# The last 96 columns of w1 join wqkv's third head block, and a table sets the order of all operations

## The chip, the cores and the metric

The kernel runs on one core of one Trainium2 chip. The metric is the device time of one execution in microseconds (us), from which the median of several runs is told. PE is TensorE, DVE VectorE, ACT ScalarE, POOL GpSimd and SP SyncE, whose queue issues every DMA of this kernel.

## The reference

With x of 2048 tokens by 512 channels, all in fp32:

```
xn = layernorm(x)                          # over the 512 channels
q, k, v = split(xn @ wqkv)                 # 32 heads of 16 channels
logits[s, w] = q[s] . k[s - 2*w] / 4       # a window of 8 keys, 2 apart; -1e9 before the start
s = softmax(logits) @ v, heads joined, @ wo
y = layernorm(xn)
g = silu(gelu(y @ w1 + b1) @ w2 + b2)      # w1: 512 x 1376, w2: 1376 x 512
out = x + s * g
```

1376 hidden channels are ten blocks of 128 and a last block of 96.

## The kernel before

**Arithmetic and tiles.** Each fp32 operand of a large product is split in two fp16 tiles, a high and a low part, and three of the four products of parts are summed, so each product takes three fp16 matmuls per 128 input channels (12 for 512). The tokens are dealt in two halves c = 0, 1 (even and odd positions), each of 8 tiles i of 128 tokens; `yT[0..3]` hold the normalised tokens transposed, 512 tokens each. The heads are taken in four head blocks hb of 8 heads, so there are eight units u = 4c + hb.

**A unit.** `qkv(c, hb, u)` (line 721) makes q, k and v of the unit: for each of the 8 token tiles, 12 matmuls with 128 tokens as the loaded operand and 384 streamed columns of `wq` (L746) fill one PSUM tile `ps`, which ACT (L763) or DVE (L759) scales into `U[u % 2]`. `attention(c, hb, u)` (line 790) works on DVE: four multiplies q by k (L805), four reductions (L808), a softmax, four multiplies by v (L863), adds on DVE (L858) and POOL (L873, L883). `U` has two buffers, so unit u+2's results can be written only after unit u's last L863.

**The channel MLP.** `mlp1(ch, f)` (line 1008) makes hidden block f for the 512 tokens of chunk ch: 12 matmuls with 128 columns of w1 loaded and 512 tokens streamed (L1016), then the gelu with its bias (ACT, L1033), the high part (ACT, L1036) and the low part (DVE, L1038). The last block f = 10 has 96 columns and goes into its own tile `hlast`, whose 97th row holds the constant for b2. Its matmuls stream 512 tokens as the others do. `mlp2(ch, f)` (line 1043) adds h times w2 into four PSUM tiles z, 3 matmuls of 512 columns each (L1052); after f = 10 ACT takes the silu (L1068), which goes to DRAM (`gd`). `mlp2` runs two steps behind `mlp1` (`LAG`).

**Start.** The first loads bring x (some tiles transposed, `xt`), wqkv of head block 0 (`stq`, in two halves) and w1. Token tiles 6 and 7 skip the normalisation for unit 0: `center` subtracts the mean, made by PE (L599) or by DVE and PE (L602, L608), and `direct` multiplies them in fp32 (L617). The others are normalised (`y0`: POOL L665, ACT L661 or DVE L668 by `Y_ENG`) and transposed by PE (L683) or, where `BYDMA` says so, by a DMA transpose (L675). 24 matmuls on a constant (L1169) fill PE meanwhile and compute nothing that is used.

**End.** `wo_last` (line 951) multiplies the second half's attention by wo: for each tile 9 matmuls over three head blocks, 3 more once the last block is there (L961). DVE multiplies by the gate (L993) and adds x (L1000; three tiles on POOL, L997), and a DMA writes the tile.

**Order.** `Plan` records every operation with what it reads and writes, and a cost. Before, `issue` (line 221) is a list scheduler: it repeatedly takes the operation that can start first by those costs, ties going by the priorities `PQ0`, `PY`, `PG` and others. Each engine runs its own list strictly in that order.

## Time and profile before

| | |
|---|---|
| median of 3 runs | 415.07 us (414.49 to 415.13) |
| the profiled execution, its own time | 415.18 us |
| its span, first to last instruction | 413.4 us, so 1.78 us lie around it |
| PE busy | 405.9 us, 98% of the span |
| DVE busy | 379.5 us, 92% |
| ACT, POOL busy | 222.1 us (54%), 120.3 us (29%) |
| mean granted PE clock | 0.999 |

A row of a timeline gives start, length, engine, line, operation, output <- input, how many instructions, and in brackets the idle time just before them and what ended it. A row of a group gives busy time, the mean of one in ns, then idle time and its releaser. Matmuls are pipelined, so the mean of one matmul in a group contains the overlap with its neighbours; their real rate is read from the chain, where a row gives the time that a run of them took.

### The profile page before, as it was taken

Reading aid. Unit: us, or ns where it says so; the run is one execution under the profiler, and the core shown is the slowest. Engines: PE = TensorE matmul, PEld = TensorE weight load, DVE = VectorE, ACT = ScalarE, POOL = GpSimd, SP = SyncE. Lnnn points to the kernel's source line nnn. Section 1 sums busy time; section 2 is a strip of 40 time slices with the busy share of each in tenths; the row PEclk is TensorE's granted clock in tenths of the full one; section 3 lists DMA queues with packets and bytes.
Section 4 is the critical chain, followed back from the end, with each engine's and each line's share of the span. In section 5 each row is a group of like instructions: output and inputs, shape, how many; then the busy total and the mean of one; then the engine's idle time right before and its main releaser. Section 6 shows DMA issues by size and latency. Waiting matters only on the chain.

```text
span 413.4 us, 5554 instructions
## 1 busy us (share of the span) xinstructions
PE 405.9 (98%) x2083; PEld 206.6 (50%) x2083; DVE 379.5 (92%) x379; ACT 222.1 (54%) x353; POOL 120.3 (29%) x131
## 2 busy tenths in 40 slices
PE   8799999999999999999999999999999999999996
PEld 5555544445654455445544554455455544444443
DVE  4996989998999999989998999999999998999954
ACT  4699899994549655843384252225212393263500
POOL 3834002004380425042504330434033404520021
PEclk9999999999999999999999999999999999999999
DMA  8958717030045137720172034223604244007133
GB/s 281 397 112 258 235 61 230 0 128 1 1 142 152 28 93 183 149 46 2 48 221 75 0 102 116 68 86 88 205 7 122 88 111 145 0 18 238 23 102 131
DMA packets 47211, 46.41 MB, mean 112 GB/s; under 512 B 31785, under 2 KB 32225, under 8 KB 46673
## 3 DMA queue, kind: packets, MB, share of 16 engines
q1 hardware_dynamic: 47184, 46.06, 37.6%
q8 instruction: 16, 0.26, 0.3%
q14 instruction: 11, 0.08, 0.1%
HBM read 24.06 MB, written 7.34 MB: 76 GB/s over the span
## 4 chain that ended last, share of the span: by engine, by line
PE 92%; ACT 3%; issue 1%; DVE 1%; POOL 1%; ACTq 0%
PE z L1052 28%; PE ps L1016 28%; PE ps L746 25%; PE ps L929 5%; PE ps L961 2%; PE z L961 2%; PE pl L746 1%; ACT w L421 1%; PE pl L961 1%; ACT f L673 1%; ACT yT L687 0%; ACT wq L536 0%; POOL wq L471 0%; POOL rb L635 0%; ACT prod L661 0%
## 5 line engine op out<-in xcount | busy, mean ns | idle before, releaser
L1016 PE MATMUL ps<-yT,w 128*128 128x512 f16 (+1 forms) x528 | 120.4, 379 | 0.0
L746 PE MATMUL ps<-wq,yT 128*128 128x384 f16 x708 | 117.0, 326 | 0.2 <-DVE U L759 0.2
L1052 PE MATMUL z<-w,h 128*128 128x512 f16 x480 | 110.4, 379 | 0.0
L746 PEld LDWEIGHTS <-yT 128*128 128x128 f16 x744 | 72.5, 98 | 49.2 <-issue 1.0
L1016 PEld LDWEIGHTS <-w 128*128 128x128 f16 (+1 forms) x528 | 52.8, 100 | 61.0
L805 DVE TENSOR_TENSOR prod<-U 128x2048 f32<-128x2048 f32 x32 | 73.2, 2286 | 2.2 <-POOL prod L883 0.7
L1052 PEld LDWEIGHTS <-h 128*128 128x128 f16 x480 | 46.6, 98 | 55.5 <-issue 0.3
L808 DVE TENSOR_REDUCE L<-prod 128x128 f32<-128x2048 f32 x32 | 73.0, 2281 | 0.4
L1033 ACT ACTIVATE ps<-ps,b1T,hsc 128x512 f32<-128x512 f32 (+1 forms) x44 | 32.9, 748 | 73.4 <-PE ps L1016 72.2
L863 DVE TENSOR_TENSOR prod<-pl,U 128x2048 f32<-128x2048 f32 x28 | 63.2, 2283 | 4.2 <-POOL prod L873 4.1
L763 ACT ACTIVATE U<-ps,cs 128x384 f32<-128x384 f32 x54 | 31.2, 580 | 65.2 <-PE ps L746 65.2
L873 POOL TENSOR_TENSOR prod<-prod,prod 128x2048 f32<-128x2048 f32 x7 | 31.7, 4531 | 113.8 <-DVE prod L863 99.6
L883 POOL TENSOR_TENSOR prod<-prod 128x1024 f32<-128x1024 f32 x14 | 32.9, 2349 | 0.0
L882 POOL COPY gate<-prod 1x1 f32<-1x1 f32 x21 | 5.5, 264 | 91.0 <-DVE prod L805 82.2
L1038 DVE SCALAR_TENSOR_TENSOR h<-ps,hsc,h 128x512 f16<-128x512 f32 x40 | 29.6, 741 | 1.7 <-ACT h L1036 1.4
L1036 ACT ACTIVATE h<-ps,hsc 128x512 f16<-128x512 f32 x40 | 27.3, 684 | 1.3 <-PE z L1052 0.4
L929 PE MATMUL ps<-wo,oT 128*128 128x512 f16 x96 | 21.7, 379 | 0.0
L858 DVE TENSOR_TENSOR prod<-prod,prod 128x2048 f32<-128x2048 f32 x9 | 20.5, 2282 | 0.0
L1033 ACT ACT_TABLE_LOAD x10 | 12.8, 1283 | 8.6 <-PE ps L1016 8.5
L883 POOL TENSOR_TENSOR prod<-prod,prod 128x1024 f32<-128x1024 f32 x7 | 16.4, 2347 | 0.0
L961 PEld LDWEIGHTS <-oT 128*128 128x128 f16 x108 | 10.6, 98 | 10.4
L929 PEld LDWEIGHTS <-oT 128*128 128x128 f16 x96 | 9.4, 98 | 11.2
(179 smaller groups left out, 377.8 us busy)
## 6 DMA issues: line engine op xcount, KB each, us to landing
f<-in_A_x_dram SPq DMA_DIRECT2D x31, 256.0 KB, 3.5
U<-U SPq DMA_DIRECT2D x16, 392.0 KB, 4.0
gd<-f SPq DMA_DIRECT2D x12, 256.0 KB, 3.4
prod<-in_A_x_dram SPq DMA_DIRECT2D x8, 256.0 KB, 6.9
oT<-in_B_w_dram SPq DMA_DIRECT2D x2, 1024.0 KB
yT<-in_B_w_dram SPq DMA_DIRECT2D x2, 1024.0 KB, 7.9
f<-gd SPq DMA_DIRECT2D x8, 256.0 KB, 2.7
out_dram<-f SPq DMA_DIRECT2D x8, 256.0 KB, 2.8
```

What stands on the lines that cost most here:

```text
L746: nc.tensor.matmul(b.t[:, 0:384], y[:, s, k, o:o + P], wq[:, hb, t, k], start=(n == 0), stop=(n == 11))
L763: act(384, lambda i=i, b=b: nc.scalar.activation(U3[:, i:i + 31:15, :], b.t[:, 0:384].rearrange("p (t e) -> p t e", t=3), AF.Identity, sca ...
L805: dve(2048, lambda p2=p2, g=g: nc.vector.tensor_tensor(p2(), q, slots(Ut, KH, 2 * g), op=ALU.mult), qk + [("kh", ub, 0), ("kh", ub, 1), (" ...
L808: dve(2048, lambda pr=pr, g=g: nc.vector.tensor_reduce(L3()[:, 2 * g:2 * g + 2], pr.t.rearrange("p (r f d) -> p r f d", r=2, d=DH), AX.X, ...
L863: dve(2048, lambda: nc.vector.tensor_tensor(pr.t.rearrange("p (r f d) -> p r f d", r=2, d=DH), A3()[:, 2 * g:2 * g + 2].rearrange("p r (f ...
L873: pool(4.75, lambda: nc.gpsimd.tensor_tensor(acc.t, acc.t, p1.t, op=ALU.add), [acc, p1], [acc])
L883: nc.gpsimd.tensor_tensor(x.t[:, 0:1024], x.t[:, 0:1024], y(), op=ALU.add)
L929: nc.tensor.matmul(b.t, oT[:, hb, i // 4, s, i % 4], wo[:, t, hb], start=(hb == 0 and n == 0), stop=(hb == last and n == 2))
L961: nc.tensor.matmul(b.t[:, cols], oT[:, hb, i // 4, s, i % 4], wo[:, t, hb, cols], start=(start and hb == 0 and n == 0), stop=(stop and hb ...
L1016: nc.tensor.matmul(b.t[0:M], w1[:, s, f * 512 + k * M:f * 512 + (k + 1) * M], yT[ch][:, t, k], start=(n == 0), stop=(n == 11))
L1033: act(512, lambda: nc.scalar.activation(b.t[0:M], b.t[0:M], AF.Gelu_apprx_tanh, bias=b1T[0:M, f:f + 1], scale=hsc[0:M, 1:2]), [b, ("b1T",) ...
L1052: nc.tensor.matmul(z.t, hl[s][0:K, t * P:(t + 1) * P], w2[0:K, w, f], start=(f == 0 and n == 0), stop=(f == NF - 1 and n == 2))
```

## The change

**The last block of w1.** `wq` becomes one tile per head block, and that of the third block (`HLAST = 2`) is 480 columns wide: 384 of wqkv and the 96 of w1. In units 2 and 6 the 12 matmuls of a token tile stream 480 columns. `mlp1` no longer runs for f = 10. Instead ACT copies the 96 extra columns of each tile out of PSUM into `hpt`, and `last_block`, once per chunk, adds the bias on POOL, takes the gelu and the high part on ACT and the low part on DVE. All this is by tokens, so a DMA transpose turns it into `hlt`, which `mlp2(ch, 10)` reads in place of `hlast`. `hlt` uses one new tile, `hl0`, and the tile `first`, where the constants of the start had been. b1 is loaded with 96 more columns.

**The order.** A table `ORDER` of 1260 numbers is followed by `issue` in place of its choice. Several settings change with it: which engine does which split, eviction or normalisation, the grouping of the first tiles, the load order, and the places of the MLP steps between units (`MLPN`).

```diff
+HLAST = 2
-BYDMA = (4, 5, 6, 7)
+BYDMA = (2, 5, 6, 7)
-Y_ENG = ('pool', 'act', 'dve', 'dve', 'act', 'pool', 'dve', 'act')
+Y_ENG = ('act', 'dve', 'act', 'dve', 'act', 'act', 'dve', 'act')
-W1ENG = ('act', 'dve', 'act', 'act', 'act', 'act', 'act')
+W1ENG = ('dve', 'dve', 'act', 'dve', 'dve', 'act', 'dve')
-W2LO = ('dve', 'dve', 'dve', 'dve', 'dve', 'pool', 'dve')
+W2LO = ('dve', 'dve', 'pool', 'pool', 'pool', 'dve', 'dve')
-MEANBY = ('dve', 'pe', 'pool', 'pool')
+MEANBY = ('pe', 'pe', 'pe', 'dve')
-MLPN = (7, 7, 6, 4, 7, 7, 2, 0)
+MLPN = (0, 12, 2, 7, 4, 11, 1, 3)
+ORDER = (
+    4, 18, 0, 2, 1, 3, 8, 36, 239, 38, 37, 39, 48, 109, 108, 31, 113, 117, 123, 120, 133, 131, 124, 118, 128,
...
-        order = []
+        order, fixed = [], [self.ops[n] for n in reversed(ORDER)]
         while len(order) < len(self.ops):
             best = None
-            for e, cand in engs.items():
+            if fixed:
+                o = fixed.pop()
+                t = max([self.earliest(o)] + [min(b.ring.free) for b in o.bufs if b.slot is None])
+                assert not o.npred and t < float("inf")
+                best = (t, o)
+            for e, cand in engs.items() if best is None else ():
...
-    wq = sb.tile([P, NHB, 2, KT, 384], F16, name="wq")
-    w1 = sb.tile([P, 2, KT * F], F16, name="w1")
+    wq = [sb.tile([P, 2, KT, 384 + FL * (hb == HLAST)], F16, name=f"wq{hb}") for hb in range(NHB)]
+    w1 = sb.tile([P, 2, W1C[3]], F16, name="w1")
+    wl = wq[HLAST][:, :, :, 384:384 + FL]
-    hlast = sb.tile([P, 2, 512], F16, name="hlast")
+    hl0 = sb.tile([P, 512], F32, name="hl0")
+    hpt = [hl0[:, 0:512], first[:, 0:512]]
+    hlt = [h.bitcast(F16).rearrange("p (a t) -> p a t", a=2) for h in hpt]
...
+    def last_block(ch):
+        n = 4 * FL
+        h16 = R_f.new()
+        v = lambda: h16.t.bitcast(F16).rearrange("p (a t f) -> p a t f", a=2, t=4)
+        j = ch % 2
+        x = hpt[j][:, 0:n]
...
+        def pads():
+            nc.gpsimd.memset(v()[:, :, :, FL:P], 0.0)
+            nc.gpsimd.tensor_scalar(v()[:, 0, :, FL], halves[:, 8:12], hsc[:, 2:3], 2.0, op0=ALU.mult, op1=ALU.mult)
+        with prio(PEV):
+            pool(0.9, pads, [("hsc2",), ("hp", j, 0), ("hp", j, 1)], [(h16, 2)], port=False)
+            pool(1.0, lambda: nc.gpsimd.tensor_tensor(x3(), x3(), row, op=ALU.add), xk + [("b1T",)], xk)
+            act(n, lambda: nc.scalar.activation(x, x, AF.Gelu_apprx_tanh), xk, xk,
+                aps=1, table="gelu")
+            act(n, lambda: nc.scalar.activation(v()[:, 0, :, 0:FL], x3(), AF.Identity, scale=hsc[:, 2:3]),
+                xk + [("hsc2",)], [(h16, 0)])
+            dve(n, lambda: nc.vector.scalar_tensor_tensor(v()[:, 1, :, 0:FL], x3(), hsc[:, 2:3], v()[:, 0, :, 0:FL],
+                                                          op0=ALU.mult, op1=ALU.subtract),
+                xk + [(h16, 0)], [(h16, 1)], c=0.125)
+            dst = hlt[ch % 2].rearrange("p a (t x) -> p (a t) x", t=4)
+            dma(P * 2048, lambda: nc.sync.dma_start_transpose(dst, h16.t.bitcast(F16)), [(h16, k) for k in range(3)],
+                [("hl", ch % 2)], rate=140e3, issue=1.3, tail=1.2)
...
+        wide = 384 + FL * (hb == HLAST)
...
-                    nc.tensor.matmul(b.t[:, 0:384], y[:, s, k, o:o + P], wq[:, hb, t, k],
+                    nc.tensor.matmul(b.t[:, 0:wide], y[:, s, k, o:o + P], wq[hb][:, t, k],
...
+            if hb == HLAST:
+                act(FL, lambda i=i, b=b: nc.scalar.activation(
+                    hpt[i // 4][:, (i % 4) * FL:(i % 4 + 1) * FL], b.t[:, 384:384 + FL], AF.Identity, scale=hsc[:, 1:2]),
+                    [b, ("hsc",)], [("hp", i // 4, i % 4)], prio=PEV, after=pl.users([("hp", i // 4, i % 4), ("hl", i // 4)]))
+        for j in range(2 if hb == HLAST else 0):
+            last_block(2 * c + j)
...
-            if p < len(steps):
+            if p < len(steps) and steps[p][1] < NF - 1:
                 with prio(PR_M + p * 10):
                     mlp1(*steps[p])
```

Three places show what the table does. Names of tiles carry a running number behind the underscore; line numbers of the changed kernel are about 75 to 110 higher.

**The start, SP.** SP's first loads before: transposed x of tile 6, wqkv of head block 0 in two halves (`prod_93`), then two plain tiles of x.

```order
L1124 DMA U_87<-in_A_xt_dram 128x512
L505 DMA prod_93<-in_A_wqkv_dram 128x768 x2
L1099 DMA prod_94<-in_A_x_dram 128x512 x2
L505 DMA U_87<-in_A_wqkv_dram 128x768
L1124 DMA U_87<-in_A_xt_dram 128x512
```

And now:

```order
L1208 DMA prod_95<-in_A_x_dram 128x512
L1242 DMA b1T<-in_B_b_dram 128x107
L1233 DMA U_89<-in_A_xt_dram 128x512 x2
L579 DMA prod_96<-in_A_wqkv_dram 128x768 x2
L1208 DMA prod_95<-in_A_x_dram 128x512
```

The first plain tile of x moved from fourth place to the first, the biases and both transposed tiles stand ahead of wqkv, and wqkv's two halves come after 823 KB instead of 256 KB.

**The start, PE.** PE's rows before around the first transposes (L683) and the first fp16 projection (L746):

```order
L1169 LDWEIGHTS fours
L1169 MATMUL z_143<-fours 128x256
L683 MATMUL z_146<-ident,prod_94 128x128 x4
L617 MATMUL z_144<-prod_93,U_87 128x384 x4
L430 LDWEIGHTS fours
L430 MATMUL ps_141<-s_124,fours 128x1
L746 LDWEIGHTS yT_82
L746 MATMUL ps_139<-wq,yT_82 128x384
```

And now, where the means (L673) of both centred tiles and the first transposes (L757) stand:

```order
L673 MATMUL ps_141<-U_89,first 128x128 x4
L673 MATMUL ps_142<-U_89,first 128x128 x4
L757 MATMUL z_148<-first,prod_95 128x128 x4
L1279 LDWEIGHTS fours
L1279 MATMUL z_145<-first,fours 128x256
```

The first transposes moved ahead of every direct matmul; the direct ones (L691) all follow these rows, and then the first fp16 projections.

**Unit 0's end, DVE.** Before, DVE's rows from the last but one multiply by v of unit 0 to the low part of the last hidden block of chunk 0 and on:

```order
L863 TENSOR_TENSOR prod_93<-pl_142,U_86 128x2048
L1038 SCALAR_TENSOR_TENSOR h_107<-ps_141,hsc,h_107 128x512
L1038 SCALAR_TENSOR_TENSOR hlast<-ps_140,hsc,hlast 96x512
L863 TENSOR_TENSOR prod_94<-pl_142,U_86 128x2048
L441 TENSOR_SCALAR s_130<-ps_139 128x1
```

Now the low part of that block (L815, of `hl`) stands in the next unit, right before unit 2's first multiply (L914):

```order
L1143 SCALAR_TENSOR_TENSOR h_108<-ps_143,hsc,h_108 128x512
L815 SCALAR_TENSOR_TENSOR f_101<-hl_93,hsc,f_101 128x4x96
L938 TENSOR_TENSOR L_106<-L_106,mx_113 128x512
L1143 SCALAR_TENSOR_TENSOR h_110<-ps_141,hsc,h_110 128x512
L634 TENSOR_SCALAR lw_134<-mv_161 128x8
L914 TENSOR_TENSOR prod_96<-U_88 128x2048
```

It moved behind the last multiply by v of unit 0, because its input now comes from unit 2's projections.

**The end, DVE.** DVE's last rows before:

```order
L1000 TENSOR_TENSOR U_86<-U_86,f_102 128x512
L993 SCALAR_TENSOR_TENSOR U_86<-z_146,osc,U_86 128x256
L1000 TENSOR_TENSOR U_86<-U_86 128x256
L993 SCALAR_TENSOR_TENSOR U_86<-ps_139,osc,U_86 128x256
L1000 TENSOR_TENSOR U_86<-U_86 128x256
```

And now:

```order
L1109 TENSOR_TENSOR U_88<-U_88,f_99 128x512
L1102 SCALAR_TENSOR_TENSOR U_88<-z_148,osc,U_88 128x256
L1109 TENSOR_TENSOR U_88<-U_88,f_104 128x512
L1102 SCALAR_TENSOR_TENSOR U_88<-ps_141,osc,U_88 128x256
L1109 TENSOR_TENSOR U_88<-U_88 128x256 x2
```

The add of the last but one piece moved behind the last multiply, and one add of a whole tile between the two multiplies.

More of the change, by code (lines that the diff above doesn't have):

```diff
@@ L360, in tile_mixer @@
     PR_H, PR_U, PR_M = 200.0, 1000.0, 1000000.0
-    ident = sb.tile([P, P], F32, name="ident")
+    first = sb.tile([P, 512], F32, name="first")
+    ident, mean1 = first[:, 0:P], first[:, P:2 * P]
     make_identity(nc, ident)
-    fours = sb.tile([P, 2 * P], BF16, name="fours")
+    fours = sb.tile([P, P], BF16, name="fours")
     nc.vector.memset(fours, 4.0)
-    mean1 = sb.tile([P, P], F32, name="mean1")
     nc.vector.memset(mean1, 1.0 / D)
@@ L1008, in mlp1 @@
     def mlp1(ch, f):
-        M = P if f < NF - 1 else FL
+        M = P
         c, j = ch // 2, ch % 2
@@ L1024, in mlp1 @@
                after=pl.users([b]))
-        if f < NF - 1:
-            h = R_h.new()
-            hi, lo = (lambda: h.t[:, 0]), (lambda: h.t[:, 1])
-        else:
-            h = ("hlast",)
-            hi, lo = (lambda: hlast[:, 0]), (lambda: hlast[:, 1])
-        hk = (h, 0) if f < NF - 1 else ("hlast", 0)
+        h = R_h.new()
+        hi, lo = (lambda: h.t[:, 0]), (lambda: h.t[:, 1])
+        hk = (h, 0)
         with prio(PR_H + pl.prio * 1e-6):
@@ L1168, in tile_mixer @@
         b = R_z[0].new()
-        pl.add("pe", 0.2, lambda b=b: nc.tensor.matmul(b.t[:, 0:2 * P], fours[:, 0:P], fours, start=True,
+        pl.add("pe", 0.2, lambda b=b: nc.tensor.matmul(b.t[:, 0:2 * P], fours, mean1.bitcast(BF16), start=True,
                                                        stop=True), [], [b], prio=1e9)
```

112 lines of the change are left out of this document (59 added, 53 removed), and 60 rows, old and new, of the table ORDER.

## The prediction

> **What bounds the kernel now.** I read the page first: engines, the slices of the span, then the chain of work that ended last.
>
> ```profile
> span 413.4 us, 5554 instructions
> PE 405.9 (98%) x2083; PEld 206.6 (50%) x2083; DVE 379.5 (92%) x379; ACT 222.1 (54%) x353; POOL 120.3 (29%) x131
> DVE  4996989998999999989998999999999998999954
> PE 92%; ACT 3%; issue 1%; DVE 1%; POOL 1%; ACTq 0%
> ```
>
> PE is busy for 405.9 of 413.4 us and carries 92% of the chain. DVE is close behind: outside the start and the end its slices are all 8s and 9s. So time leaves only with PE work or with a PE wait, and DVE decides how much of it can leave. A middle stretch shows both (columns: PE, PEld, DVE, ACT, POOL busy):
>
> ```profile
> 150.00:200.00 50.00, 50.00 (x265) 26.07 (x264) 47.41 (x35) 27.36 (x44) 17.17 (x17) 1.00 0.38 82
> ```
>
> PE has no gap there; DVE has 2.6 us in 50. Where are PE's 7.5 us without work? The timeline of the start and of the end gives nearly all of them:
>
> ```profile
> 1.18 3.38 PE L1169 MATMUL z<-fours 128*128 128x256 bf16 x15 [1.18 <-DVE fours L365]
> ...
> 12.86 0.66 PE L683 MATMUL z<-ident,prod 128*128 128x128 f32 x4 [1.65 <-POOL prod L665]
> ...
> 17.84 1.85 PE L683 MATMUL z<-ident,prod 128*128 128x128 f32 x12 [0.40 <-DVE prod L668]
> ...
> 24.44 5.36 PE L746 MATMUL ps<-wq,yT 128*128 128x384 f16 x32 [0.19 <-DVE U L759]
> ```
>
> ```profile
> 408.29 1.47 PE L961 MATMUL ps<-wo,oT 128*128 128x256 f16 x12
> ...
> 409.80 0.48 DVE L993 SCALAR_TENSOR_TENSOR U<-ps,osc,U 128x256 f32<-128x256 f32 x1 [0.29 <-PE ps L961]
> 410.32 0.42 DVE L1000 TENSOR_TENSOR U<-U 128x256 f32<-128x256 f32 x1
> ```
>
> 1.2 us before the first matmul, 1.65, 0.40 and 0.19 of waits (2.2 together), and 3.6 us from PE's end (408.29 + 1.47) to the span's end; 0.5 us is in crumbs. The profiled execution took 415.18 us, 1.78 more than its span and 0.11 more than the median of 415.07. I reckon against 415.18.
>
> **PE work removed and added.** The chain gives clean rates:
>
> ```profile
> 98.36 2.59 PE ps L1016 x12
> ...
> 101.60 15.60 PE ps L746 x96
> ```
>
> Twelve matmuls of 512 columns take 2.59 us (215.8 ns each), 96 of 384 take 15.60 (162.5 each). The last hidden block is its own group, with as many columns streamed as any other block:
>
> ```profile
> L1016 PE MATMUL ps<-yT,w 128*96 128x512 f16 x48 | 11.0, 379 | 0.0
> ```
>
> These 48 go: 48 x 0.2158 = 10.36 us. In their place 192 matmuls (two units, 8 tiles, 12 each) grow from 384 to 480 columns. That width does not occur in the trace. Its neighbours bound it: at 162.5 ns the growth is free, at 215.8 it costs all of 192 x 53.3 ns = 10.2 us. On the line between them 480 columns are 162.5 + 96/128 x 53.3 = 202.5 ns, so +40.0 x 192 = 7.7 us. I take that, since both rows lie on one rate per column (0.42 ns). Net: **-2.7 us**.
>
> Both centred tiles now take their mean on PE, before one was prepared by DVE:
>
> ```profile
> 3.57 1.02 DVE L602 TENSOR_REDUCE f<-U 128x128 f32<-128x512 f32 x1 [2.29 <-DMA U<-in_A_xt_dram]
> ...
> 4.65 0.79 PE L608 MATMUL ps<-f,mean 128*128 128x128 f32 x2
> ...
> 9.83 1.16 PE L599 MATMUL ps<-U,mean 128*128 128x128 f32 x8
> ```
>
> +1.16 - 0.79 = **+0.4 us** of PE. The rest of PE's work has the same count, the 24 idle matmuls too. PE's sum becomes 405.9 - 2.7 + 0.4 = 403.6.
>
> **The tail.** The table puts the last multiply (0.48), then two adds of 0.42, after PE's end, where one add stood; a whole-tile add is squeezed in just ahead. Between one more add (0.4) and that plus part of the whole-tile add (0.7), with nothing as the lower end if the DMAs hide it: I take **+0.5**, so 4.1.
>
> **The floor.** 403.6 + 1.2 before the first matmul + 0.5 crumbs + 4.1 tail = 409.4 us of span, 411.2 us of time. To it comes x, all that PE waits in between; x was 2.2 before. The forecast is a forecast of x, and 4.0 us of it would eat the whole gain.
>
> **x in the start.** Before, PE waited longest for the first normalised tile, which POOL made slowly:
>
> ```profile
> 8.80 0.68 DVE L576 BATCH_NORM_STATS2 bn<-prod 128x6 f32<-128x512 f32 x1
> ...
> 10.05 0.57 POOL L635 TENSOR_TENSOR rb<-pb,halves 128x1 f32<-128x1 f32 x1 [5.94 <-DVE pb L633]
> ...
> 10.73 2.08 POOL L665 TENSOR_SCALAR prod<-prod,mv,rb 128x512 f32<-128x512 f32 x1
> ...
> 17.86 0.28 ACT L659 ACTIVATE rb<-pb,rb 128x1 f32<-128x1 f32 x1
> ...
> 18.18 0.81 ACT L661 ACTIVATE prod<-prod,rb 128x512 f32<-128x512 f32 x1
> ```
>
> Now that tile is loaded first and ACT does it in 0.28 + 0.81, so it is ready near 7 us, not at 12.8: the first load ended DVE's wait at 3.57, statistics and scale take 1.8 (8.80 to 10.62), ACT 1.1, and the hand-overs a few tenths. This wait goes. Late next is wqkv, behind 823 KB instead of 256:
>
> ```profile
> 6.84 0.84 ACT L514 ACTIVATE wq<-prod 128x768 bf16<-128x768 f32 x1 [1.41 <-DMA prod<-in_A_wqkv_dram]
> ...
> 15.96 0.81 PE L746 MATMUL ps<-wq,yT 128*128 128x384 f16 x4
> ...
> 5.00:10.00 5.00, 4.88 (x20) 2.76 (x20) 2.97 (x11) 2.44 (x7) 0.00 (x0) 1.00 0.99 358
> ```
>
> ACT got its second half at 6.84, when 1,024 KB had been asked for, itself included; now it is 1,591 KB. At the 358 GB/s of that stretch (its last column) the 567 KB more are 1.6 us; if the DMA engines were not full before, 0 to 1. I take 1. All direct matmuls (16 in the trace's count, 6 us) then follow in one piece, and the first L746 starts near 15 us against 15.96, with less left to do behind it. I give the start x = 0.8 (bounds 0.2 and 3): the old wait gone, a smaller one new.
>
> **x in the middle.** DVE's work must not grow, since it has 5% of air. L602 goes (1.0); the four low parts keep their count and shrink from 512 to 384 elements (744 to 608 ns: 0.5 less); two more halves of w2 go to POOL (2 x 1.28 less), two smaller ones come off (1.2 less); w1's splits bring one low part (1.28) and 2.8 us of high parts. In sum about **-1 us**: DVE's path shortens by less than PE's.
>
> ```profile
> L1038 DVE SCALAR_TENSOR_TENSOR hlast<-ps,hsc,hlast 96x512 f16<-96x512 f32 x4 | 3.0, 744 | 1.9 <-ACT hlast L1036 1.9
> L486 DVE SCALAR_TENSOR_TENSOR w<-yT,zsc,w 128x1024 f16<-128x1024 f32 x4 | 4.9, 1280 | 0.0
> L486 DVE SCALAR_TENSOR_TENSOR w<-h,hsc,w 128x384 f16<-128x384 f32 x1 | 0.6, 608 | 0.0
> L480 DVE TENSOR_SCALAR w<-oT,hsc 128x512 f16<-128x512 f32 x1 | 0.5, 486 | 0.0
> ```
>
> ACT's 16 copies of 96 columns and three more table loads (1.28 each) lie in its 46% of idle time. The block's new chain (copy, POOL's add, gelu, high, low, DMA transpose) is on PE's path only if `mlp2` of f = 10 comes before it lands. Chunks 1, 2 and 3 have 50 us of other PE work or more between the last 480-column matmul and that `mlp2`. Chunk 0 has 14. DVE is the longest part there: from unit 0's last L863 to the low part stand three multiplies, three reductions, an add of that size (7 x 2.28) and 13.6 us of shorter work, 29.6 in all; the transpose adds 3.3 from issue to landing. PE, from the first 480-column matmul to the first matmul that needs the block, has 8 tiles of 2.43 and 75 matmuls of 512 columns, 35.6 us.
>
> ```profile
> 98.47 2.28 DVE L863 TENSOR_TENSOR prod<-pl,U 128x2048 f32<-128x2048 f32 x1
> ...
> L805 DVE TENSOR_TENSOR prod<-U 128x2048 f32<-128x2048 f32 x32 | 73.2, 2286 | 2.2 <-POOL prod L883 0.7 <-DMA U<-U 0.3
> L808 DVE TENSOR_REDUCE L<-prod 128x128 f32<-128x2048 f32 x32 | 73.0, 2281 | 0.4
> yT<-f SPq DMA_TRANSPOSE x12, 3.3
> ```
>
> Unit 0's last L863 ended at 100.75, 0.85 us before unit 2's first L746 at 101.60. With that lead kept, the block lands 35.6 - 32.9 + 0.9 = 3.6 us ahead of need. I give the middle x = 1.0, between 0 and 6. Together **x = 1.8**.
>
> **Sum.** 411.2 + 1.8 = **413.0 us**, 0.5% below 415.07.
>
> **A rule weighed.** A rival price for the new POOL work comes from DVE. It is tested by two rows that overlap from 22.04 to 22.62, POOL's scale and a DVE subtract that reads two SBUF tiles:
>
> ```profile
> 20.54 2.08 POOL L665 TENSOR_SCALAR prod<-prod,mv,rb 128x512 f32<-128x512 f32 x1
> ...
> 22.04 0.68 DVE L674 TENSOR_TENSOR f<-prod,f 128x512 f16<-128x512 f32 x1
> 24.55 0.69 DVE L674 TENSOR_TENSOR f<-prod,f 128x512 f16<-128x512 f32 x1
> ```
>
> The subtract took no longer than its twin at 24.55. The Trainium skill, "SBUF — State Buffer", section "Who interferes with whom", says otherwise: such a pair shares a port, and the later one blocks until the first is done. By that rule the block's POOL adds could each stop a DVE multiply for their whole length. This trace does not show it.
>
> **The rivals.**
> - *No waits at all* (x under 0.8): DVE follows and the start is clean. 411.2 to 412.0. Against it: before, x was 2.2. Chance 0.15.
> - *Forecast*, x from 0.8 to 3.0, 412.0 to 414.2: 0.47.
> - *DVE sets the pace, or the change does not do what it says*: PE's 2.7 us return as waits on DVE, which got only 1 us shorter: 415.18 - 1.0 + 0.5 = 414.7. Or 480 columns cost as much as 512: +2.5, 415.5. For it: DVE's 47.41 in 50. Against: PE waited nowhere in the middle before. 0.14, at 414.2 to 415.9.
> - *Slower, by chunk 0's block.* PE takes its list strictly, so if DVE's low part or SP's queue (halo copies stand ahead of the transpose) delays the block, `mlp2`, then `mlp1` and unit 3's projections stand still, and DVE runs dry behind them. It waits from 3.6 us of delay on, and costs one for one; from 6.5 us on (413.0 + 2.9) the result is over 415.9. With 8 us late, 417.4. A DVE block for each POOL operation there would do it: add 0.93, two w2 pairs of 3.5 each make 7.9. Chance 0.18.
> - *Slower in the start*: wqkv 3 us or more late, x = 5: 416.2. Chance 0.06.
>
> **How the numbers follow.** Forecast 413.0, the likeliest case. Low end 411.0, just under the floor; high end 417.0, which leaves out about a tenth of the slow cases and reaches through both unknown costs. A measurement tells about 0.2% from no change, here 414.24 and 415.90. Faster: 0.15 + 0.47 = 0.62. Same 0.14. Slower 0.18 + 0.06 = 0.24.
>
> **What would show it.** Right: runs of 96 matmuls of 480 columns at 19.4 us; PE busy near 403.6; the first transposes near 7 us; PE without a gap over 0.5 us between 40 and 390; DVE's idle there shrinking. Wrong: PE idle before the `mlp2` of the first transposed block, put down to a DMA; a PE wait on ACT's first L514 beyond 1 us; DVE rows of L914 longer than 2.29 where POOL works; a tail over 4.3 us.

## The result, and the profile after

The changed kernel takes **418.07 us** (median of eight executions, 415.88 to 419.50) against 415.04 us before (eight, 414.49 to 415.18): ratio 1.0069, 95% interval 1.0045 to 1.0093. It is 0.7% slower, and its executions lie 3.6 us apart where those before lay 0.7 apart. The profiled execution took 417.76 us.

Page of the changed kernel: span, busy time, DVE's slices, and the chain of work that ended last.

```profile
span 416.0 us, 5478 instructions
PE 403.0 (97%) x2041; PEld 200.8 (48%) x2041; DVE 381.2 (92%) x381; ACT 225.6 (54%) x372; POOL 134.9 (32%) x145
DVE  4988999999989999999999998999999979998974
PE 67%; DVE 20%; issue 4%; DMA 3%; ACT 2%; POOL 1%; SPq 1%; DVEq 0%; ACTq 0%
```

PE works 2.9 us less than before, as meant. But the chain, 92% PE before, now runs through DVE for a fifth of the span, in stretches that end where PE waits for DVE. The chain also prices the new width:

```profile
104.28 9.72 PE ps L848 x48
```

48 matmuls of 480 columns in 9.72 us are 202.5 ns each. All waits of PE (the second row is the 1.2 us before its first matmul):

```profile
PE ps L673 <- DMA U<-in_A_xt_dram: 1.3, 2, 0.8
PE z L1279 <- DVE first L438: 1.2, 1, 1.2
PE ps L1125 <- DVE f L1052: 1.1, 1, 1.1
PE z L757 <- DVE prod L742: 0.7, 1, 0.7
PE ps L848 <- DVE h L1143: 0.6, 1, 0.6
PE ps L848 <- ACT yT L761: 0.6, 1, 0.6
PE ps L1125 <- DVE h L1143: 0.5, 1, 0.5
```

L673, L757 and the ACT row are the start: 2.55 us, ending at 5.17, 6.79, 16.84 and 18.55. The three others are the middle, 2.28 us, ending at 56.56, 184.63 and 296.76, all on DVE, and before there was none. How little air DVE has shows the same stretch as before (columns: PE, PEld, DVE, ACT, POOL busy):

```profile
150.00:200.00 50.00, 49.36 (x263) 25.59 (x262) 48.85 (x34) 25.23 (x43) 15.31 (x16) 1.00 0.45 94
```

DVE 48.85 of 50, before 47.41, and PE 49.36 instead of 50.00. Now the end. First the timeline of the changed kernel, then what its SP queue waited for from 400 us on:

```profile
401.72 11.03 SPq L1111 DMA_DIRECT2D out_dram<-U  x9
...
407.80 1.47 PE L1070 MATMUL ps<-wo,oT 128*128 128x256 f16 x12
...
409.72 0.75 DVE L1109 TENSOR_TENSOR U<-U 128x256 f32<-128x256 f32 x2
```

```profile
SPq L1111 <- DVE U L1109: 5.6, 2, 4.1
SPq L1111 <- POOL U L1106: 2.6, 1, 2.6
```

PE ends at 409.27 and DVE at 410.47, both earlier than before (409.76, 410.74), yet the span ends at 416.0 instead of 413.4: **6.7 us behind PE's end instead of 3.6**. SP takes its list of nine stores strictly: the second is issued at 404.77 and the third, which waits 4.1 us for one of the last adds, at 409.28, while four finished tiles stand behind it. The last two columns of the windows (share of the DMA engines, GB/s) show where the stores then run. Before:

```profile
408.00:412.00 4.00, 1.76 (x17) 1.34 (x14) 2.38 (x5) 0.00 (x0) 0.00 (x0) 1.00 0.36 129
412.00:416.00 4.00, 0.00 (x0) 0.00 (x0) 0.00 (x0) 0.00 (x0) 0.00 (x0) 0.64 0.01 4
```

After:

```profile
408.00:412.00 4.00, 1.28 (x12) 0.89 (x10) 2.40 (x6) 0.00 (x0) 0.00 (x0) 1.00 0.48 180
412.00:416.00 4.00, 0.00 (x0) 0.00 (x0) 0.00 (x0) 0.00 (x0) 0.00 (x0) 0.75 0.59 214
```

The forecast's sum and the profiled execution, term by term:

| term | forecast | measured |
|---|---|---|
| PE busy | 403.6 | 403.0 |
| before the first matmul | 1.2 | 1.2 |
| PE waits, start | 0.8 | 2.55 |
| PE waits, middle | 1.0 | 2.28 |
| crumbs | 0.5 | 0.2 |
| behind PE's end | 4.1 | 6.7 |
| around the span | 1.78 | 1.76 |
| time | 413.0 | 417.76 |

Tail +2.6, start +1.75, middle +1.3 make 5.6; PE and the crumbs give back 0.9.

### The profile page after: what moved, and what is told of

It is laid out like the page before. It is cut to its first block, busy times and chain, and to the rows that moved or that the text cites. A ratio compares the mean times of both kernels' runs of the same rounds, so it can differ in the third digit from the quotient of the medians.

```text
span 416.0 us, 5478 instructions
## 1 busy us (share of the span) xinstructions
PE 403.0 (97%) x2041; PEld 200.8 (48%) x2041; DVE 381.2 (92%) x381; ACT 225.6 (54%) x372; POOL 134.9 (32%) x145
## 4 chain that ended last, share of the span: by engine, by line
PE 67%; DVE 20%; issue 4%; DMA 3%; ACT 2%; POOL 1%; SPq 1%; DVEq 0%; ACTq 0%
PE z L1161 23%; PE ps L848 20%; PE ps L1125 18%; DVE prod L972 4%; DVE L L917 4%; DVE prod L914 3%; PE ps L1070 2%; PE z L1070 2%; DVE h L1143 1%; DMA U<-U 1%; DMA U<-in_A_xt_dram 1%; DVE f L1029 1%; DMA out_dram<-f 1%; PE pl L848 1%; DVE f L787 1%
## 5 line engine op out<-in xcount | busy, mean ns | idle before, releaser
L848 PE MATMUL ps<-wq,yT 128*128 128x384 f16 (+1 forms) x720 | 129.7, 337 | 1.3 <-DVE h L1143 0.6
L1161 PE MATMUL z<-w,h 128*128 128x512 f16 x480 | 112.8, 379 | 0.0
L1125 PE MATMUL ps<-yT,w 128*128 128x512 f16 x480 | 110.3, 379 | 1.6 <-DVE f L1052 1.1
L848 PEld LDWEIGHTS <-yT 128*128 128x128 f16 x744 | 72.2, 98 | 59.5 <-issue 1.5
L914 DVE TENSOR_TENSOR prod<-U 128x2048 f32<-128x2048 f32 x32 | 73.0, 2286 | 2.4 <-DMA U<-U 1.1
L1125 PEld LDWEIGHTS <-w 128*128 128x128 f16 x480 | 46.8, 98 | 57.7 <-issue 2.5
L982 POOL TENSOR_TENSOR prod<-prod,prod 128x2048 f32<-128x2048 f32 x7 | 34.1, 4876 | 85.8 <-DVE prod L972 66.2
L1138 ACT ACTIVATE ps<-ps,b1T,hsc 128x512 f32<-128x512 f32 x40 | 29.7, 747 | 36.0 <-PE ps L1125 35.5
L967 DVE TENSOR_TENSOR prod<-prod,prod 128x2048 f32<-128x2048 f32 x9 | 20.6, 2286 | 0.1
```

The costliest lines, as they stand in the source:

```text
L848: nc.tensor.matmul(b.t[:, 0:wide], y[:, s, k, o:o + P], wq[hb][:, t, k], start=(n == 0), stop=(n == 11))
L914: dve(2048, lambda p2=p2, g=g: nc.vector.tensor_tensor(p2(), q, slots(Ut, KH, 2 * g), op=ALU.mult), qk + [("kh", ub, 0), ("kh", ub, 1), (" ...
L982: pool(4.75, lambda: nc.gpsimd.tensor_tensor(acc.t, acc.t, p1.t, op=ALU.add), [acc, p1], [acc])
L1125: nc.tensor.matmul(b.t[0:M], w1[:, s, f * 512 + k * M:f * 512 + (k + 1) * M], yT[ch][:, t, k], start=(n == 0), stop=(n == 11))
L1138: act(512, lambda: nc.scalar.activation(b.t[0:M], b.t[0:M], AF.Gelu_apprx_tanh, bias=b1T[0:M, f:f + 1], scale=hsc[0:M, 1:2]), [b, ("b1T",) ...
L1161: nc.tensor.matmul(z.t, hl[s][0:K, t * P:(t + 1) * P], w2[0:K, w, f], start=(f == 0 and n == 0), stop=(f == NF - 1 and n == 2))
```

## The experiments

The theory T: the streaming of the block is the gain on PE that was forecast, and three things of the table and the loads eat it: SP's order of the stores, the order of the loads, the places of some DVE operations. The rival R: the block's own chain (copies, adds, transposes) and the new settings cost it, wherever they stand. Later came C and J, on what sets the start and the spread of the executions (C: PE's clock, still at half after a gap; J: loads that land earlier or later), and P, on a port that DVE and POOL share.

Kernels that edit the table do it by a list of moves: operation a goes right ahead of b, and only the order on the engine of a changes.

```diff
+MOVE = ((1225, 1220), (1230, 1250), (1240, 1250), (1245, 1250))
...
-        order, fixed = [], [self.ops[n] for n in reversed(ORDER)]
+        seq = list(ORDER)
+        for a, b in MOVE:
+            seq.remove(a)
+            seq.insert(seq.index(b), a)
+        order, fixed = [], [self.ops[n] for n in reversed(seq)]
```

That makes six more lines: L848 of the changed kernel is L854 in theirs, and so on; in e2 and e3, which have no table, L848 is L786, and e4 has the lines of the kernel before. All times, each with its ratio to the kernel before on the same chip (medians there 414.85 to 415.06):

| kernel | median us (from, to) | ratio, 95% interval |
|---|---|---|
| e1 stores in order | 415.82 (413.0, 417.1) | 1.0011 [0.9995, 1.0026] |
| e2 no table | 415.31 (413.75, 418.21) | 1.0013 [0.9996, 1.0031] |
| e3 block, old settings, no table | 425.54 (425.18, 426.51) | 1.0258 [1.0244, 1.0271] |
| e4 no block, new settings | 420.18 (420.0, 420.31) | 1.0126 [1.0113, 1.0139] |
| e5 e1 + idle matmuls ahead | 414.93 (413.3, 417.88) | 1.0000 [0.9982, 1.0018] |
| e6 e1 + two DVE operations | 414.41 (411.88, 415.09) | 0.9971 [0.9957, 0.9986] |
| e7 e1 + bias load late | 414.20 (412.47, 416.6) | 0.9984 [0.9966, 1.0002] |
| e8 all of these | 413.04 (412.59, 414.18) | 0.9959 [0.9947, 0.9971] |
| e9 e8, idle matmuls back | 412.56 (411.63, 412.92) | 0.9938 [0.9926, 0.9949] |
| e10 e8, 18 idle matmuls left out | 414.57 (413.0, 418.38) | 0.9985 [0.9969, 1.0001] |
| e11 e8, block late | 422.66 (421.22, 424.54) | 1.0190 [1.0167, 1.0212] |
| e12 the change again | 417.78 (416.81, 419.69) | 1.0071 [1.0054, 1.0088] |
| e13 e1 + three adds ahead | 414.24 (412.64, 415.85) | 0.9981 [0.9968, 0.9994] |
| e14 e9 + three adds ahead | 411.76 (411.0, 413.77) | 0.9931 [0.9912, 0.9950] |
| e15 e14, table's tail | 414.69 (413.8, 416.05) | 0.9994 [0.9985, 1.0003] |

### The tail alone (e1)

The edit is the list of moves above, four of SP's stores.

> Edit: SP issues the last nine output stores in the order in which their sums become ready (tiles 3, 1, 0, 2, 5, 4, 6, then the two halves of 7); nothing else of the table is touched. Theory T (the changed kernel loses 3.1 us behind PE's end because SP, which takes its list strictly, has nothing to do from 404.8 to 409.3 and then issues seven stores in a row): the span ends 2.6 to 3.0 us earlier, the time falls from 418.1 to 415.1-415.5, and PE's end (near 409.3) stays. Rival R1 (the end is set by DVE's last adds or by the store bandwidth of 380-395 GB/s, whatever the order): less than 0.8 us, 417.3 or more.

Measured: 415.82 us, 2.25 less than the change and a little above T's range. In the profile of e1:

```profile
402.45 9.28 SPq L1117 DMA_DIRECT2D out_dram<-U  x9
...
408.53 1.47 PE L1076 MATMUL ps<-wo,oT 128*128 128x256 f16 x12
```

PE ends at 410.00 and the span at 414.3: 4.3 us instead of 6.7. R1 is out: with the same adds and the same bytes the span ends 2.4 us sooner behind PE's end. One more thing stands in this profile. The centring on PE (L673 there, L679 here) is first the changed kernel's, then e1's:

```profile
5.17 1.16 PE L673 MATMUL ps<-U,first 128*128 128x128 f32 x8 [0.82 <-DMA U<-in_A_xt_dram]
```

```profile
5.48 3.78 PE L679 MATMUL ps<-U,first 128*128 128x128 f32 x16 [1.14 <-DMA U<-in_A_xt_dram]
```

The same matmuls at 145 ns there and 236 here, and the first projections at 14.36 there and 15.90 here. That gave theory C below.

### Table, settings and block apart (e2, e3, e4)

e2 sets `ORDER = ()`: the planner's list scheduler decides. e3 does that too and takes all settings of the kernel before. e4 is the kernel before with the new settings.

> Edit: the table is empty, so that the planner's list scheduler picks the order from the same ops, settings and priorities; the last block stays beside wqkv. Theory T (the streaming of the last block is a gain of 2.7 us on PE and the table's order spoils it): stores are issued by readiness, the tail is about 3.6-4, PE busy stays near 403, and the time is 413.5 to 416.5, below the changed kernel's 418.1. Rival R2 (the order is not to blame, the block's new chain and the new settings cost the 3 us wherever they are put): 417.5 or more. A third possibility: the settings are made for the table and the scheduler does worse with them, over 419.

> Edit: the last block beside wqkv, but the table empty and all settings (loads, engines of the copies, priorities, order of tiles, units of the MLP) those of the kernel before. Theory T: only the streaming of the block is left of the change, PE busy falls by about 2.9 us and the waits stay near those before: 412.5 to 414.0. Rival R2 (the block's chain costs what it saves: 16 copies on ACT, four POOL adds and pads, four DMA transposes, a later w1 for the third head block): 415.0 or more, with PE waits before the second product of the first transposed block.

> Edit: the kernel before (last block in matmuls of its own, no table) with the settings of the changed kernel. Theory T: the settings move the start (first transposes near 8 us), PE busy stays near 406, and the time is within 1.5 us of 415.0, either side. Rival R2 (settings are harmless and the block is what costs): 413.5 to 414.5. If the new settings themselves cost (tables of engines that load DVE more): over 416.5.

e2, without the table, is 2.8 us below the change, where T put it, so the table's order does cost. Its fastest execution took 413.75; the profiled one 418.21, and shows why (the third number from the right is PE's granted clock):

```profile
20.00:24.00 4.00, 2.88 (x11) 1.84 (x12) 3.87 (x8) 3.93 (x9) 0.12 (x1) 0.54 0.81 234
24.00:28.00 4.00, 4.00 (x17) 2.00 (x16) 2.89 (x6) 3.85 (x5) 0.00 (x0) 0.61 0.04 4
```

For 8 us PE had little over half its clock, 3.4 us lost ((0.46 + 0.39) x 4), behind waits of 0.67, 0.50 and 1.47 us between 17 and 21 us.

e3 was expected at 412.5 to 414.0 and took 425.54: a plain miss. PE waited 2.15 us at 64.67, 1.96 at 67.00 (w2's split not made) and 3.69 at 139.61 on DVE, and the clock followed:

```profile
64.00:68.00 4.00, 1.37 (x4) 0.49 (x4) 4.00 (x4) 4.00 (x5) 0.17 (x2) 0.73 0.03 5
68.00:72.00 4.00, 4.00 (x11) 1.32 (x9) 4.00 (x5) 2.81 (x6) 2.86 (x2) 0.50 0.84 256
```

Waits 7.8, clock 3.4 here and 1.7 again at 140: 415.0 - 2.9 + 12.9 = 425.0. The block alone does not do this, since e2 has it without these waits. That the old settings make w2 and w1 in an order that suited other due times is an argument; no run shows it. So e3 doesn't say what the block costs, only that it can't be dropped into the old order. e4 missed too (420.18, expected within 1.5 of 415.0): PE busy 406.6, start waits of 3.9 us, 6.5 us behind PE's end. Of the 4.9 us between e4 and e2 the tail is 2.6 (3.9 in e2), so at most 2.3 speaks for the block. R's simple form (settings harmless, block dear) has lost here; the sizes are not clean.

### Start, middle, and all moves together (e5 to e9)

On top of e1: e5 moves six idle matmuls ahead of the centring; e6 two DVE operations (859 keeps its place on PE); e7 the bias load behind w1's loads. e8 has all, and the first half of the last tile's add one place ahead with its store; e9 is e8 without the idle matmuls' moves.

```diff
+# e5
+    (126, 19), (122, 19), (114, 19), (132, 19), (130, 25), (125, 25)
+# e6
+    (859, 942), (860, 942), (742, 615)
+# e7
+    (18, 17)
+# e8
+    (1254, 1249), (1255, 1250)
```

> Edit, on top of the reordered stores: six of the 24 idle matmuls move in the table, four ahead of the first centring on PE and two ahead of the second, so that PE has no gap between 1.2 and 7 us. Theory C (the run-to-run scatter of 413.0 to 417.1 us and part of the lost time come from PE's clock: with a gap of 0.8 to 1.1 us before the centring PE is still at half clock at 5.5 us in most executions, 236 ns per 128-column f32 matmul against 145, and the critical start is 1.5 us later): the 16 centring matmuls take 1.2 + 1.2 us in the profile, the median falls by 1 to 2 us from 415.8, and the runs lie within 1.5 us of each other. Rival J (jitter of the loads' landing): median and scatter stay as they were, 415 to 416.5 with 3 us or more between the ends. The third possibility, that the idle matmuls delay the centring: up to 0.5 us later.

> Edit, on top of the reordered stores: two DVE operations move ahead in the table, the low part of one hidden block by one place (it frees the PSUM bank for which the projections wait at 184.6 us) and one eviction of the first output product by five places (bank awaited at 296.8). Nothing changes on PE, ACT, POOL and SP. Theory T (in the middle PE waits only on DVE's order, 0.64 and 1.10 us): both waits are gone and the median is 414.0 to 414.6 against 415.8. Rival D (DVE is the bound there and a wait taken away comes back behind): 415.4 or more, with new PE waits of the same sum.

> Edit, on top of the reordered stores: the load of the biases (128 rows of 428 bytes), second in SP's list, moves behind the w1 loads. Theory S (it holds the two transposed tiles back by its issue of 0.45 us): the first centring starts 0.4 to 0.5 us earlier, the median is 415.2 to 415.5. Rival: the transposed tiles land no earlier since the data of the first tile is ahead of them, or the clock decides: 415.6 to 416.

> Edit: the reordered stores, the idle matmuls, the two DVE operations and the bias load of the other three kernels together, and one small add with its store one place ahead at the end. If the causes are separate (tail, start clock, DVE order), they add up: 415.8 - 1.5 - 1.5 - 0.4 = 412.4, between 411.9 and 413.3, below the kernel before (415.0); PE busy near 403, waits of PE under 2.5 in all. Rival: they share one cover (an earlier start only lets DVE's chain wait less on PE), 413.8 or more.

> Edit: the kernel with all moves, but the six idle matmuls back at their places. Theory C (PE's clock in the start costs time in most executions): the bias load no longer holds the first transposed tile, so the gap before the centring is short (under 0.3 us) and little is left for the idle matmuls to save: 413.0 to 413.8. Rival J (the loads alone decide): 412.4 to 413.2, no worse than with them, since they only fill PE.

**e6**: 414.41, 1.4 below e1, as T expected. This is the place at 296 us in the changed kernel; the second row is an eviction whose matmuls had ended by 289.7 us, when PE went on to the next group, and PE's wait ends with it:

```profile
295.44 0.61 DVE L815 SCALAR_TENSOR_TENSOR f<-first,hsc,f 128x384 f16<-128x384 f32 x1
295.96 0.75 DVE L1052 SCALAR_TENSOR_TENSOR f<-ps,osc,f 128x512 f32<-128x512 f32 x1
...
296.76 0.59 PE L1125 MATMUL ps<-yT,w 128*128 128x512 f16 x2 [1.10 <-DVE f L1052]
```

In e6 this eviction stands five places ahead, and neither this wait nor that at 184.63 is left in the list; a new one of 0.34 us stands at 305. DVE is close to the bound but the order was what cost: D is out for these two places.

**e7**: 414.20, 1.6 below e1 by the medians and 1.1 by the ratios, more than expected. SP's first rows in the changed kernel, then in e7, where the transposed tiles follow at once:

```profile
1.21 0.41 SPq L1242 DMA_DIRECT2D b1T<-in_B_b_dram  x1
1.66 0.91 SPq L1233 DMA_DIRECT2D U<-in_A_xt_dram  x2
```

```profile
1.21 0.88 SPq L1239 DMA_DIRECT2D U<-in_A_xt_dram  x2
...
4.23 2.61 PE L679 MATMUL ps<-U,first 128*128 128x128 f32 x16
```

The issue moved by 0.45 us, the first centring from 5.17 to 4.23, by 0.94; PE doesn't wait for it at all. The rest may be the data of the 128 short rows; that was not isolated. Nor was the clock: without the gap before it, the centring also takes 2.61 us instead of e1's 3.78.

**e5** is unclear: 0.9 below e1 by the medians, intervals that overlap, and a spread as wide as e1's, where C expected 1.5 us. **e8** and **e9** settle it: with the idle matmuls ahead 413.04, without 412.56. The idle matmuls gain nothing once the bias load is out of the way; the time without them is at the low end of J's range. Both are faster than the kernel before.

### What a cold or waiting PE costs (e10, e11)

e10 leaves 18 idle matmuls out. e11 delays the first chunk's block, the rival of the prediction, by moving it on DVE.

```diff
+# e10
+COLD = (0, 2, 3, 4, 5, 7, 8, 10, 11, 12, 13, 14, 16, 17, 18, 21, 22, 23)
...
-        pl.add("pe", 0.2, lambda b=b: nc.tensor.matmul(b.t[:, 0:2 * P], fours, mean1.bitcast(BF16), start=True,
-                                                       stop=True), [], [b], prio=1e9)
+        pl.add("pe", 0.2, lambda b=b, n=n: n in COLD or nc.tensor.matmul(
+            b.t[:, 0:2 * P], fours, mean1.bitcast(BF16), start=True, stop=True), [], [b], prio=1e9)
+# e11
+    (466, 337), (468, 337), (431, 337), (432, 337)
```

> Edit: the kernel with all moves, but the first 18 of the 24 idle matmuls are not issued, so that PE does nothing before the first transposed tile lands near 4.2 us. They compute nothing that is used. Theory C: PE comes to the centring at half clock, the 16 matmuls of 128 columns take 3.8 us (236 ns each) instead of 2.4, the first direct matmuls too are slow until about 10 us, and the time is 1.2 to 2.5 us over the 413.0 of all moves. Rival J (clock in the start is off the path, loads and DVE decide): within 0.5 us of 413.0.

> Edit: the kernel with all moves, but DVE makes the low part of the first chunk's last block behind one multiply of 2.28 us and 6 us of shorter work more than before, so that its DMA transpose lands near 132.6 us, 5.7 us after PE reaches the second product that reads it (126.9). This is the prediction's rival made to happen. Theory: PE stands still 5.7 us there, and DVE does not make it up: 413.0 + 5.7 = 418.7, plus up to 3.4 us if the clock halves behind the gap as it did in the kernel with the old settings: 418.5 to 422. Rival: other waits later in the run absorb part of it, 415 to 417.

e10 took 414.57, 1.5 more than e8, and its executions spread over 5.4 us:

```profile
4.22 2.05 PE L680 MATMUL ps<-U,first 128*128 128x128 f32 x8 [4.22 <-DVE mv L658]
```

256 ns per matmul: PE comes cold to the centring. It is on the path: PE's last wait of the start ends at 19.39 instead of 18.04 in e8, 1.35 us later. The rest of this execution, the slowest of e10, lies elsewhere:

```profile
56.47 0.17 PE L516 MATMUL z<-s,fours 128*128 128x5 bf16 x1 [2.22 <-ACT w L502]
```

ACT had waited 2.24 and 1.15 us for loads of weights just before, and behind PE's wait the clock was at half for 3.41 us. So C is right on the price of a cold PE. Whether PE comes cold goes with the gap that the loads leave, in the five profiles with one start: 0.82, 0.89 and 1.04 us without the slow centring (the changed kernel, e6, e12), 1.14 and 1.12 with it (e1, e13). No run varies that gap alone.

e11 took 422.66, 9.6 more than e8, a little over the range:

```profile
135.60 5.28 PE L1167 MATMUL z<-w,hl 97*128 97x512 f16 x12 [5.89 <-DMA hl<-f]
```

```profile
132.00:136.00 4.00, 0.40 (x2) 0.16 (x3) 2.58 (x2) 0.40 (x1) 1.28 (x1) 0.89 0.35 66
136.00:140.00 4.00, 4.00 (x11) 1.49 (x10) 0.42 (x1) 1.19 (x2) 3.22 (x1) 0.50 0.00 0
140.00:144.00 4.00, 4.00 (x16) 1.58 (x14) 2.47 (x2) 3.05 (x7) 0.00 (x0) 0.76 0.53 131
```

The wait is put to the block's DMA as the prediction said it would be, 5.89 us; behind it the clock is at half, (0.11 + 0.50 + 0.24) x 4 = 3.4 us more. 5.9 + 3.4 = 9.3 of the 9.6 between the medians (the profiled execution, at 424.38, lost 1.7 us of clock at 19 as well). Nothing absorbs it. The mechanism existed; the change just didn't run into it.

### DVE and POOL (e12, e13), and the sum (e14, e15)

> The changed kernel itself once more, nothing edited, for the spread of its runs and a second look at its start. Theory C: the profiled execution has the 16 centring matmuls either at 145 ns (first projections near 18.5 us) or at 236 ns (near 20.1), and the middle wait at 56 us comes with the early start only; runs again over 2.5 us or more, median 417 to 418.5, the tail 6.5 to 6.9 us. Rival J: the centring always at 145 ns, and the spread comes with the landing of the loads.

e12 took 417.78, again 2.9 us from end to end, with the tail at 6.7. Neither profile of this kernel has the slow centring, but e1 and e13, which start with the same list, have it: C is not out for the spread. The transposed tiles landed later than in the first profile (centring at 5.39 and 7.50), which speaks for J. But DVE was busy for 379.0 us here and 381.2 in the first profile, and the wait of 1.10 us at 297 was missing. The two differ at one place. The changed kernel first:

```profile
270.61 4.17 DVE L1029 TENSOR_TENSOR f<-f,f 128x512 f32<-128x512 f32 x3
270.75 0.58 POOL L991 COPY gate<-prod 1x1 f32<-1x1 f32 x1 [11.82 <-DVE prod L914]
271.29 2.33 POOL L992 TENSOR_TENSOR prod<-prod 128x1024 f32<-128x1024 f32 x1
```

The same in e12:

```profile
271.76 1.89 DVE L1029 TENSOR_TENSOR f<-f,f 128x512 f32<-128x512 f32 x3
271.91 1.78 POOL L991 COPY gate<-prod 1x1 f32<-1x1 f32 x1 [11.82 <-DVE prod L914]
...
273.65 2.35 POOL L992 TENSOR_TENSOR prod<-prod 128x1024 f32<-128x1024 f32 x1
```

Three adds of 0.68 us, each with two tiles in SBUF. In the first execution POOL's add gets in between and one of the three takes 2.97 us, until POOL is done; in the second the adds go through and POOL's copy of one element (0.17 us elsewhere) is held for 1.78. In all ten profiles that keep these places POOL's copy starts 0.14 to 0.15 us behind the first add, whichever way it goes, so these rows don't show what decides. e13 puts the three ahead of the multiply for which POOL's copy waits.

```diff
+    (837, 925), (843, 925), (849, 925)
```

> Edit, on top of the reordered stores alone: the three adds of the first output tiles on DVE move ahead of the multiply before which POOL waits for its gate copy, so that they no longer meet POOL's add at 270-274 us. Theory P (a DVE operation with two SBUF inputs and a POOL add stop each other; in some executions the second of the three adds takes 2.97 us instead of 0.68, DVE's sum is 381 and PE waits 1.10 us at 297, in others 379 and no wait): the profile shows L1035 near 0.69 us for all eight, DVE near 379.0 and no PE wait at 297; the median is 0.3 to 0.9 us under the 415.8 of the reordered stores, the spread a little smaller. Rival J (start only): 415.5 to 416, the wait at 297 still there.

414.24, 1.6 below e1 by the medians and 1.2 by the ratios, more than was expected. In its profile the meeting is gone:

```profile
L1035 DVE TENSOR_TENSOR f<-f,f 128x512 f32<-128x512 f32 x8 | 5.5, 706 | 0.1
```

DVE is busy for 379.2 us, and PE has no wait at 297. Across the 13 profiles with the table, this group's mean is 706 to 708 ns in six (three of them with the adds ahead), with DVE's sum at 378.9 to 379.2, and 989 to 992 in seven, with 380.3 to 381.3; and where 860 still stands at its old place the 1.1 us at 297 come only with it. But the spread stayed at 3.2 us: P explains the wait and the two sums, not the spread.

> Edit: the kernel with all moves but the idle matmuls (412.56 us), and the three adds ahead as well. Theory P: DVE near 379.0 in every execution, no PE wait of 0.35 us at 305: 412.2 to 412.6. If the adds ahead hold POOL back (its gate opens 1.9 us later): 412.6 to 413.5.

> Edit: the same as the kernel with all moves, the adds ahead and the idle matmuls at their places, but the last adds and stores in the order of the changed kernel's table. Theory T (the tail is a cost of its own, whatever lies ahead): 2.2 to 2.8 us more than that kernel, 414.6 to 415.3, with 6.5 us or more from PE's end to the span's end. Rival: part of the tail was hidden by the later end of PE, under 1.5 us more.

e14, e9 with the adds ahead, has the lowest median: 411.76, **0.7% faster than the kernel before** (0.9931, 0.9912 to 0.9950). It is not clear of e9, whose interval overlaps. e15 gives it back the table's tail: 414.69, 2.9 more, with 6.7 us behind PE's end (406.62 to 413.3). The tail is a cost of its own: 2.25 with the table's start and middle ahead of it, 2.9 with the changed ones.

So 418.07 comes apart: by the medians stores 2.25, bias load 1.6, two DVE operations 1.4, adds against POOL 1.6; by the ratios of the table 2.4, 1.1, 1.7 and 1.2. Each was measured alone (the last three on e1), with some 0.9 us of uncertainty. They don't simply add: the wait of 1.10 us at 297 goes with the DVE operations as well as with the adds, and behind e9 the adds bring 0.8 by the medians and 0.3 by the ratios, within the noise. The sum of the medians, 6.9, would leave 411.2; all together gave 411.76.

Still open is the spread: executions of e14 differ by 2.8 us. The profiles show two things that vary from execution to execution, and no run isolates either. One is the clock at the start. The trace's record of the clock has its first entry of full speed at 4.40 us in the first profile, 4.72 in e12 and 4.91 in e6, but at 10.43 in e1 and 9.13 in e13, all with the same lists at the start; the first projections start at 14.36, 15.07 and 13.70 there, 15.90 and 15.81 here. The other is a load of 1 MB of weights issued between 39 and 43 us: it lands 7.0 to 7.9 us later in ten of the 13 profiles with the table, and 9.8, 10.1 and 12.0 us later in e12, e15 and e10. Those three are the ones in which PE waits behind ACT's work on it, for 0.71, 1.04 and 2.52 us in all.

## Why the prediction was wrong, step by step

- *PE's sum falls by 2.7 and rises by 0.4*: right. 403.0 us measured, 403.6 forecast; 480 columns cost 202.5 ns, the value taken between the neighbours.
- *The tail, "between one more add (0.4) and that plus part of the whole-tile add (0.7)", +0.5*: **this step failed, and most**: +3.1 in the profile, 2.25 to 2.9 by e1 and e15. DVE was even done earlier than before. The bound was built from DVE's instructions alone; SP's list of stores, which the table reorders too, was not walked against the times at which the sums become ready. The upper end of 0.7 had no support. Without these 2.6 us over the forecast the profiled execution would have taken 415.2, much as the kernel before.
- *The start, x = 0.8 (bounds 0.2 and 3)*: mis-sized, 2.55. The first transposes came at 7.79 (forecast near 7) and the first projections at 14.36 (near 15), both about right. "Late next is wqkv" was not: half of the waits are for the transposed tiles, behind a bias load of 55 KB that the sum of the bytes let vanish. e7 gets 1.1 to 1.6 us back by moving that load alone.
- *The middle, x = 1.0 (0 to 6)*: mis-sized, 2.28. The trace of before said that DVE has 2.6 us of air in 50; the change took more than half of it. Two of the three waits were two DVE operations a few places too late (e6); the third, at 56.56, came and went between executions.
- *DVE's work shrinks by about 1 us*: it rose by 1.7 in the profile and fell by 0.5 in e12. The counts were right, the durations not, because of the next step: summed over all DVE rows, the time beyond the median of rows of the same kind (where it is over 0.12 us) is 3.7 us before, 6.7 in the first profile and 4.3 in e12, and each of these rows overlaps one of POOL. Without it DVE's work shrank by 1.3 and 1.1 us, an estimate from these sums.
- *The rule weighed, on DVE and POOL sharing a port*: the Trainium skill was right where it matters here, and the reading of the trace too wide. "SBUF — State Buffer", "Who interferes with whom", says that a DVE instruction with two SBUF inputs and a POOL instruction that reads SBUF exclude each other, and that whoever comes first keeps the other waiting for its whole length. The add of 2.97 us above agrees, and so do the rows below. One pair without a block had been taken as the trace's answer. That pair stands (e3 has another: a subtract of 0.66 us at 20.82 beside POOL's scale of 19.20 to 21.27), and no run here explains it. The rows with blocks were there, in the spread within a group instead of its typical member. Here L560's split of wo, which now meets POOL's add for the block, with the mean of two in the third field; after, then before:

```profile
L560 DVE SCALAR_TENSOR_TENSOR wo<-yT,osc,wo 128x1024 f16<-128x1024 f32 x2 | 3.2, 1656 | 0.9 <-ACT wo L556 0.9
```

```profile
L486 DVE SCALAR_TENSOR_TENSOR wo<-yT,osc,wo 128x1024 f16<-128x1024 f32 x2 | 2.6, 1298 | 0.0
```

  And in the kernel before, one L713 of eight took 1.52 us instead of 0.68, until POOL's add of 136.74 to 141.29 was done:

```profile
136.74 4.55 POOL L873 TENSOR_TENSOR prod<-prod,prod 128x2048 f32<-128x2048 f32 x1 [14.00 <-DVE prod L863]
...
140.32 1.52 DVE L713 TENSOR_TENSOR f<-f,f 128x512 f16<-128x512 f32 x1
```

  The changed kernel has a longer one in the same group, in both of its profiles, and the chain that ended last runs through it for 2.42 us; no run moves it alone:

```profile
148.06 2.33 POOL L992 TENSOR_TENSOR prod<-prod 128x1024 f32<-128x1024 f32 x1
148.44 2.51 DVE L787 TENSOR_TENSOR f<-f,f 128x512 f16<-128x512 f32 x1
```

  The multiplies that the prediction feared for, L914, kept their mean of 2286 ns.

- *Chunk 0's block lands 3.6 us ahead of need*: right in kind. Its transpose was issued at 122.38 and takes 3.1, so it landed near 125.5 and was read at 128.09, 2.6 ahead; PE's stretch from the first 480-column matmul at 92.57 to there is 35.5 us, forecast 35.6. The slower rival built on it did not happen. Had it, it would have cost more than one for one (e11).
- *Rivals*: both slower ones named a single large wait with its place. What came was several costs of 1 to 2.9 us each, at the stores, the loads, DVE's order and the port, and neither rival stood at the tail, where the largest was.

## What to carry to other kernels

When an order is rewritten, walk every strict list, the DMA queue's too, against the times at which its entries become ready; the engine that ends last need not be the one whose list got worse. With a second engine at 95% of the first, a position in its list is worth as much as an instruction. And judge a rule on interference by the longest members of a group, with what ran beside them, before a typical row is taken as an answer.

## What the hardware showed that was not expected

- A wait of PE can cost more than itself. Every stretch at half clock between the start and PE's end lasts 3.41 or 6.83 us in these traces, so it costs 1.7 or 3.4 us. It was 6.83 with a gap of 5.89 us (e11), with two of 2.15 and 1.96 and 0.4 us of work between them (e3) and with three of 0.67, 0.50 and 1.47 between 17 and 21 us (e2); it was 3.41 with one of 3.69 (e3) and with 2.22 and 0.30 in a row (e10). Gaps of up to 1.1 us in the middle of the changed kernel left it at 1.00. Near 18 us gaps of 1.12 and 0.61 halved it for 3.41 in e11, and gaps of 1.11 and 0.61 did not in e8. The Trainium skill, "TensorE: Matmul & The Clock Gate", "Part 1: The HAM clock gate (the "warmup" mystery)", has the clock at half after an idle window of about 3.4 us. e11 and the single gap in e3 agree; e2, e10 and the two gaps in e3 show that shorter gaps close together are enough.
- At the start the granted clock of a window reads 1.00 while the durations say half: 14 idle matmuls of 256 columns take 3.15 us (225 ns each) at 1.20, and 236 to 256 ns per f32 matmul of 128 columns where 145 is the later value. The clock's record begins with its first entry of full speed, at 4.40 us in the changed kernel and 10.43 in e1, and the durations fit that entry: before it they are to be believed, not the column.
- The order in which POOL and DVE reach their shared port differs between executions of one program, though POOL's copy starts 0.14 to 0.15 us behind the first add in all of them, and moves DVE's sum by 2.2 us.
